# Attention's q, k and v over 128 partitions, block maxima as an operand of their own, GpSimd a pair ahead

## The chip, the core and the metric

The kernel runs on one core of one Trainium2 chip. The metric is the device time of one execution in microseconds (us), as the median of three runs. A core has TensorE (matmuls and transposes into PSUM), VectorE, ScalarE and GpSimd, each with its own queue of instructions, and SyncE, which here only issues DMAs. In rows of the profile they are called PE (with PEld for its weight loads), DVE, ACT, POOL and SP (SPq, POOLq: DMAs that they issue).

## What is computed

Three layers follow one another, all in fp32. The attention is sparse: each query sees the keys nearer than 16 positions, and one summary of each block of 32 keys.

```
B, H, S, D = 2, 8, 768, 64;  block, window = 32, 16;  nb = S // block
k_sum = k.reshape(B, H, nb, block, D).max(axis=3)
v_sum = v.reshape(B, H, nb, block, D).mean(axis=3)
scores_l = where(|i - j| < window, scale * q @ k.T, -1e9)
scores_s = scale * q @ k_sum.T + log(block)
a = softmax(concat[scores_l, scores_s]);  out = a @ concat[v, v_sum]
```

Its output (1536 rows of 512) goes through a mixture of experts that sends each row to one of 8 experts (relu between 512x1024 and 1024x512 weights), and that output through a layer `(g * cos(g)) @ w_out` with `g = x @ w_in` (512x2048 and 2048x512).

## The kernel before, in words

**The attention loop.** A pair is one batch with two heads; there are 8, four for each batch. The loop `for i in range(NH + 2)` runs over halves: half i works on pair p = i // 2, on its first 384 queries where i is even and its last where i is odd, and it overlaps stages of neighbouring halves. What each half issues, in this order (`manual_schedule`: every engine gets its instructions in the order in which the code is written):

- Even halves prepare the keys of the next pair (`prep_k`), odd ones its queries (`prep_q`). GpSimd has first reordered the loaded tile so that two heads lie side by side (`shuffle`); TensorE transposes it (tiles `pk`, `pq`); `evac_k` on ScalarE copies the windows of 96 keys for each tile of 64 queries into `kb`, and VectorE takes the block maxima `ks` from PSUM, which VectorE or GpSimd copies behind every window of `kb` (24 columns, 12 times).
- `attn_scores`: 12 matmuls of 64 queries by 96 keys and 24 maxima, then on VectorE the masked sum (`s`) and its negated maximum (`nmx`). Odd halves also multiply the value sums `va`, which GpSimd makes with three additions (`prep_v1`), for the means `vsm`.
- `attn_av` for half i - 2: products with the values, and on VectorE three operations on `rs` that divide by the sums into `xb` or `big`.
- `attn_aT` for half i - 1: six transposes into `pa`, copied by ScalarE into `aT`. Then `attn_exp` for half i: six exponentials on ScalarE.

`q`, `k` and `v` are loaded by SyncE's queue in tiles of 96 partitions with 8 rows each. There is one buffer for each; a load is issued when the reorder has read the tile before.

**Around it.** `PLAN` is a string that names, for each half and each place in it (0, p, s, c, h, e), pieces of other work: the router of the first batch (A, B, P, K, C, M, T, Q), the scatter of its rows to DRAM (Z, in half 12), and the start of the experts (W, X, from half 14). `ON_VECTOR` names copies that VectorE does in place of ScalarE or GpSimd, `EARLY` the halves in which GpSimd's work is issued ahead of the scores. When half 17 is done, the experts run (`moe_first`, `moe_window`, 7 windows), with the second batch's router between, and then the last layer (`ffn_tile`). `keep_warm` issues matmuls on zeros.

Of the kernel before, what the change touches and what calls it, by code (L numbers as in the profile page):

```python
# [34 lines left out]
QP = 96  # L35
QJ = S // QP
# [15 lines left out]
ON_VECTOR = "e2 k4 k6 k8 k12 k14 x2 x3 x5"  # L52

EARLY = (2, 12)
# [20 lines left out]
C_MASK = C_VIND + NB  # L75
# [4 lines left out]
def shape_constants():  # L80
# [4 lines left out]
    c[np.arange(QP), C_VIND + np.arange(QP) // (BLK // QJ)] = 1.0 / BLK  # L85
# [19 lines left out]
def fused_kernel(ctx, tc, q, k, v, emb, tau, w1, w2, w_in, w_out, consts, out):  # L105
# [31 lines left out]
    def load_raw(b, g, raw, which="qkv"):  # L137
        h0 = 2 * g
        for w in which:
            src, off = dict(q=(q, 0), k=(k, 2), v=(v, 0))[w]  # L140
            nc.sync.dma_start(
                raw[w + "n"][off:off + QP],
                src[b, h0:h0 + 2].rearrange("h (p j) d -> p h (j d)", p=QP),
            )
# [19 lines left out]
    def shuffle(raw, n, scale, ap, eng, r=None):  # L164

        if r is None:
            r = ap.tile([P, QJ, 2, D], F32, tag="shuf", name="shuf", bufs=1)
        r = r[0:n]
        eng.tensor_scalar(
            r.rearrange("p j h d -> p h j d"), raw.rearrange("p h (j d) -> p h j d", d=D),  # L170
            scale, 1.0, op0=ALU.mult, op1=ALU.mult,
        )
        return r

    def prep_q(bf, qs, ps_t, eng):
# [24 lines left out]
    def prep_k(bf, kr, pks, ap, eng, copy_first=False):  # L200

        kb = bf["kb"]
        n = QJ // len(pks)
        for j in range(QJ):
            nc.tensor.transpose(
                pks[j // n][:, j % n, 0:QP + 4], kr[:, j].rearrange("p h d -> p (h d)"),
                ident[0:QP + 4, 0:QP + 4],
            )
        ks = ap.tile([P, 2, NB], F32, tag="ks", name="ks")
        for m, pk in enumerate(pks):  # L210
            if copy_first:
# [9 lines left out]
        eng.tensor_scalar(  # L221
            kb[:, :, KW:KC], ks[:, 0].unsqueeze(1).to_broadcast([P, NT, NB]),
            1.0, 1.0, op0=ALU.mult, op1=ALU.mult,
        )

    def prep_v1(bf, ap, eng):
        v4 = bf["vn"].rearrange("p h (j d) -> p h j d", d=D)
        va = ap.tile([QP, 2, 4, D], F32, tag="va", name="va", bufs=1)
        eng.tensor_tensor(va, v4[:, :, 0:4, :], v4[:, :, 4:8, :], op=ALU.add)
        eng.tensor_tensor(va[:, :, 0:2, :], va[:, :, 0:2, :], va[:, :, 2:4, :], op=ALU.add)  # L230
        eng.tensor_tensor(va[:, :, 0, :], va[:, :, 0, :], va[:, :, 1, :], op=ALU.add)
        return va
# [20 lines left out]
    def attn_scores(half, bf, ps_s, ap, va=None):  # L253
        qT, kb = bf["qT"], bf["kb"]
# [3 lines left out]
        for u in range(NU // 2):  # L258
            for hh in range(2):
                for m in range(2):  # L260
                    t = NU * half + 2 * u + m
                    hp = slice(64 * hh, 64 * hh + 64)
                    nc.tensor.matmul(
                        ps[64 * m:64 * m + 64, hh, u * KC:(u + 1) * KC],
                        lhsT=qT[hp, t * 64:(t + 1) * 64], rhs=kb[hp, t, :],
                        start=True, stop=True,
                    )
        pv = ps[KW:KC, 0, 3 * KC:3 * KC + 2 * D].rearrange("p (h d) -> p h d", h=2)
# [723 lines left out]
    with ExitStack() as actx:  # L992
# [26 lines left out]
        for i in range(2):  # L1019
            s = dict(  # L1020
                raw,
                vw=[ap1.tile([P, 2, NU, D + 1], F32, name=f"vw{i}{h}") for h in range(2)],
                qT=ap1.tile([P, S], F32, name=f"qT{i}"),
                kb=ap1.tile([P, NT, KC], F32, name=f"kb{i}"),
# [18 lines left out]
        load_raw(*pairs[0], raw, "k")  # L1043
        load_raw(*pairs[0], raw, "q")
        load_raw(*pairs[0], raw, "v")
        nc.sync.dma_start(csa, consts[:, C_VIND:])

        def q_room():
            r = xp.tile([P, 2 * ROW], F32, tag="xw", name="qr", bufs=3)
            return r[:, 0:2 * QJ * D].rearrange("p (j h d) -> p j h d", j=QJ, h=2)  # L1050


        kr = shuffle(
            raw["kn"], QP + 4, 1.0, ap, nc.vector,
            sets[1]["kb"].rearrange("p t c -> p (t c)")[:, 0:2 * QJ * D].rearrange(
                "p (j h d) -> p j h d", j=QJ, h=2
            ),
        )
        load_raw(*pairs[1], raw, "k")
        qs = shuffle(raw["qn"], QP, SCALE, ap, nc.vector)  # L1060
        load_raw(*pairs[1], raw, "q")
        load_vw(*pairs[0], 0, sets[0]["vw"][0])
# [6 lines left out]
        prep_k(sets[0], kr, two_banks(), ap, nc.gpsimd)  # L1069
        prep_q(sets[0], qs, ps_t, nc.vector)  # L1070
        keep_warm(6, P)
        va = prep_v1(raw, ap, nc.vector)
        load_raw(*pairs[1], raw, "v")
        kr = shuffle(raw["kn"], QP + 4, 1.0, ap, nc.gpsimd)
        load_raw(*pairs[2], raw, "k")
        qs1 = shuffle(raw["qn"], QP, SCALE, ap, nc.gpsimd, q_room())
        load_raw(*pairs[2], raw, "q")
        load_vw(*pairs[0], 1, sets[0]["vw"][1])

# [78 lines left out]
        for i in range(NH + 2):  # L1158
            def prep_qv():
                nonlocal qs, va  # L1160
                qs = shuffle(raw["qn"], QP, SCALE, ap, nc.gpsimd, q_room())
                va = prep_v1(raw, ap, nc.vector if f"v{i}" in on_vector else nc.gpsimd)
                if p + 2 < NPR:
                    load_raw(*pairs[p + 2], raw, "qv")

# [10 lines left out]
            if i == 7:  # L1176
                zt = xp.tile([P, ROW], F32, tag="junk", name="zt")
# [9 lines left out]
            if nx is not None and not odd and i > 2:  # L1187
                pk = ps_t.tile([P, QJ, P], F32, tag="tr", name="pk")
                prep_k(
                    nx, kr, [pk], ap, nc.vector if f"k{i}" in on_vector else nc.gpsimd,  # L1190
                    f"e{i}" in on_vector,
                )
# [3 lines left out]
            if i in EARLY:  # L1196
                prep_qv()
# [6 lines left out]
            if i == 0:  # L1204
                prep_v3(sets[0], means_v(va))
                va = prep_v1(raw, ap, nc.gpsimd)
                load_raw(*pairs[2], raw, "v")
                load_vw(*pairs[1], 0, sets[1]["vw"][0])
            if i == 1:
                prep_q(nx, qs1, ps_t, nc.scalar)  # L1210
# [228 lines left out]
```

## Time and profile before

| | |
|---|---|
| median of 3 runs | 539.37 us (537.84 to 540.14) |
| the profiled execution | 539.12 us, its span 537.3 us |
| TensorE busy | 506.7 us, 94% of the span |
| VectorE, ScalarE, GpSimd busy | 404.3, 304.0, 107.6 us |
| granted TensorE clock, mean | 0.984 |
| first expert's first matmul | at 97.98 us |

The span runs from the first instruction to the last; the execution has 1.8 us more around it. Busy shares are means over the attention (to about 97 us, every engine with gaps) and the two dense layers behind it, where TensorE has none.

### The profile page before, as it was taken

What the parts mean: (1) busy time and instruction counts of PE and PEld (TensorE: products, weight loads), DVE (VectorE), ACT (ScalarE), POOL (GpSimd) and SP (SyncE); (2) the same over time, 40 slices, a digit from 0 to 9 for tenths busy, and PEclk for the clock granted to TensorE, in tenths of its full rate; (3) what the DMA queues carried; (4) which work ended last, traced back from release to release, by engine and by line L of the source; (5) the groups of instructions that cost most, each with busy time, mean ns of one, the idle gap of its engine ahead of it and who ended that gap; (6) DMA issues with size and microseconds to landing.
All of it is one profiled execution on the core that took longest, in us unless ns stands there. A gap on an engine that the chain in (4) does not pass through costs nothing. (4 is left out here: it accounts for less than half of the span.)

```text
span 537.3 us, 10198 instructions
## 1 busy us (share of the span) xinstructions
PE 506.7 (94%) x3748; PEld 459.7 (86%) x3748; DVE 404.3 (75%) x834; ACT 304.0 (57%) x642; POOL 107.6 (20%) x134
## 2 busy tenths in 40 slices
PE   7879977899999999999999999999999999999993
PEld 6657656679999999999999999999999999999992
DVE  5689784898768688889779998976699765655562
ACT  2778865997656556566557675633364433333330
POOL 3787574751534000000000000000000000001222
PEclk9999986999999999999999999999999999999998
DMA  8999747787797566766304433220010000001111
GB/s 213 243 206 253 176 109 254 266 285 244 247 333 259 160 209 219 234 197 199 119 2 137 138 117 119 78 79 0 1 40 2 1 0 1 0 2 59 60 59 63
DMA packets 47688, 72.31 MB, mean 135 GB/s; under 512 B 21256, under 2 KB 21512, under 8 KB 47632
## 3 DMA queue, kind: packets, MB, share of 16 engines
q1 hardware_dynamic: 44800, 62.11, 39.6%
q0 software_dynamic: 2832, 9.49, 5.0%
q8 instruction: 31, 0.51, 0.4%
q14 instruction: 25, 0.20, 0.1%
HBM read 64.22 MB, written 7.37 MB: 133 GB/s over the span
## 5 line engine op out<-in xcount | busy, mean ns | idle before, releaser
L720 PE MATMUL po<-sl,gt 128*128 128x512 f32 x567 | 139.8, 391 | 0.0
L720 PEld LDWEIGHTS po<-sl,gt 128*128 128x128 f32 x567 | 105.5, 188 | 18.2
L720 PE MATMUL ph<-yT,sl 128*128 128x384 f32 x576 | 107.7, 336 | 0.0
L720 PEld LDWEIGHTS ph<-yT,sl 128*128 128x128 f32 x576 | 101.2, 188 | 3.7
L630 DVE TENSOR_TENSOR sl<-raw,sl 128x512 fp32r<-128x512 f32 x112 | 75.0, 706 | 11.3 <-ACT sl L629 10.9
L973 POOL DMA_INDIRECT out_dram<-acc,perm x12 | 12.0, 998 | 345.1 <-DVE acc L1349 342.6
L720 PE MATMUL py<-ht,sl 128*128 128x256 f32 x576 | 73.8, 284 | 0.0
L629 ACT ACTIVATE sl<-raw 128x512 fp32r<-128x512 f32 x112 | 63.5, 625 | 17.5 <-PE py L720 12.3
L720 PE MATMUL ph<-xT,sl 128*128 128x256 f32 x576 | 72.3, 282 | 1.0 <-DVE ht L816 1.0
L720 PEld LDWEIGHTS ph<-xT,sl 128*128 128x128 f32 x576 | 69.7, 188 | 2.4 <-DVE ht L816 1.4
L720 PEld LDWEIGHTS py<-ht,sl 128*128 128x128 f32 x576 | 70.4, 188 | 0.9 <-issue 0.6
L930 ACT ACTIVATE u<-u 128x384 f32<-128x384 f32 x64 | 33.6, 525 | 62.9 <-DVE u L929 62.8
L934 ACT ACTIVATE gt<-t 128x384 fp32r<-128x384 f32 x63 | 33.0, 524 | 31.3 <-DVE t L933 31.1
L926 ACT ACTIVATE t<-ph 128x384 f32<-128x384 f32 x64 | 31.3, 488 | 31.6 <-PE ph L720 31.2
L933 DVE TENSOR_TENSOR t<-ph,u 128x384 f32<-128x384 f32 (+1 forms) x66 | 35.8, 544 | 17.7 <-ACT u L930 17.5
L935 DVE TENSOR_TENSOR gt<-t,gt 128x384 fp32r<-128x384 f32 x63 | 35.1, 557 | 17.2 <-ACT gt L934 16.6
L928 DVE TENSOR_SCALAR u<-t 128x384 f32<-128x384 f32 x64 | 23.0, 359 | 27.7 <-ACT t L926 27.2
L929 DVE TENSOR_TENSOR u<-t,u 128x384 f32<-128x384 f32 x64 | 35.6, 557 | 1.1
L720 PE MATMUL ph<-yT,early 128*128 128x384 f32 x192 | 36.1, 338 | 0.2 <-DVE yT L1296 0.2
L720 PEld LDWEIGHTS ph<-yT,early 128*128 128x128 f32 x192 | 33.9, 188 | 1.7 <-DVE yT L1296 0.5
L284 ACT ACTIVATE s<-s,nmx 128x120 f32<-128x120 f32 x96 | 29.0, 385 | 2.6 <-DVE nmx L279 1.5
L815 ACT ACTIVATE ht<-ph 128x256 fp32r<-128x256 f32 x48 | 17.8, 378 | 15.9 <-PE ph L720 15.9
(189 smaller groups left out, 652.8 us busy)
## 6 DMA issues: line engine op xcount, KB each, us to landing
raw<-in_moe_w_dram SPq DMA_DIRECT2D x56, 512.0 KB, 4.1
raw<-in_moe_w_in_dram SPq DMA_DIRECT2D x16, 512.0 KB, 3.7
raw<-in_moe_w_out_dram SPq DMA_DIRECT2D x16, 512.0 KB
vw<-in_v_dram SPq DMA_DIRECT2D x32, 120.0 KB, 6.1
xw<-xs POOLq DMA_DIRECT2D x6, 516.0 KB
kn<-in_k_dram SPq DMA_DIRECT2D x8, 384.0 KB, 4.6
qn<-in_q_dram SPq DMA_DIRECT2D x8, 384.0 KB, 5.0
vn<-in_v_dram SPq DMA_DIRECT2D x8, 384.0 KB, 5.8
```

Source lines behind the costliest of these rows:

```text
L284: nc.scalar.activation(s[:, u, :], s[:, u, :], AF.Exp, bias=nmx[:, u:u + 1])
L629: nc.scalar.activation(sl[:, 0, c], r, AF.Copy)
L630: nc.vector.tensor_tensor(sl[:, 1, c], r, sl[:, 0, c].bitcast(F32), op=ALU.subtract)
L720: nc.tensor.matmul(acc, lhsT=lw(a), rhs=lx(c), start=(first and i == 0), stop=(last and i == 2))
L815: nc.scalar.activation(ht[:, 0], ph, AF.Relu)
L926: nc.scalar.activation(t, ph, AF.Copy, scale=1.0 / TWO_PI, bias=0.25)
L928: nc.vector.tensor_scalar(u, t, ROUND, -ROUND, op0=ALU.add, op1=ALU.add)
L929: nc.vector.tensor_tensor(u, t, u, op=ALU.subtract)
L930: nc.scalar.activation(u, u, AF.Sin, scale=TURN)
L933: nc.vector.tensor_tensor(g, ph[:, cs], u[:, cs], op=ALU.mult)
L934: nc.scalar.activation(gt[:, 0], g, AF.Copy)
L935: lo = nc.vector.tensor_tensor(gt[:, 1], g, gt[:, 0].bitcast(F32), op=ALU.subtract)
```

## The change

- q, k and v are loaded over 128 partitions with 6 rows each (768 = 128 * 6), k and v into two buffers each and q into three, and the reorders write tiles of their own (`kr`, `qs`, `va`). GpSimd's reorders and sums are issued for pair p + 2 where the prepared pair is p + 1, and the next loads behind them.
- The transposed keys go into one copy `kT` of 768 columns with 16 zero columns at either end. A tile's window is a slice of it (`kT[hp, t * 64:t * 64 + KW]`), so the scores are 12 matmuls by 96 columns.
- The block maxima are taken from `kT` in SBUF into `ks`, which is the operand of six further matmuls of 128 queries by 24 columns each half. No copy of them is made.
- The scale of q is applied in the copy out of PSUM, not in the reorder. For pair 0, keys and queries aren't reordered: 12 matmuls with the identity turn each.
- The value sums are one addition of neighbouring rows, and three matmuls where there was one.
- ScalarE gets the exponentials of half i ahead of `aT` of half i - 1. `qT` of halves 3, 5, 7 and 13 is copied by VectorE; `kT` by ScalarE in all halves but the first two, where VectorE and ScalarE take half each. Zeros for the padding rows (`zt`) move from half 7 to half 10.

`PLAN` stays.

```diff
-ON_VECTOR = "e2 k4 k6 k8 k12 k14 x2 x3 x5"
-
-EARLY = (2, 12)
+ON_VECTOR = "q3 q5 q7 q13 x2 x3 x5"
...
+    def turn_heads(dst, src, j, raw):
+
+        if not raw:
+            nc.tensor.transpose(dst, src[:, j].rearrange("p h d -> p (h d)"), ident)
+            return
+        for hh in range(2):
+            nc.tensor.matmul(
+                dst[64 * hh:64 * hh + 64], lhsT=src[:, hh, j * D:(j + 1) * D], rhs=ident,
+                start=True, stop=True,
+            )
+
+    def natural(dst, pk, j0, j1, scale, eng):
+
+        dst = dst.rearrange("d (p j) -> d p j", j=QJ)[:, :, j0:j1]
+        src = pk.rearrange("d j p -> d p j")
+        if eng is nc.scalar:
+            nc.scalar.activation(dst, src, AF.Copy, scale=scale)
+        else:
+            eng.tensor_scalar(dst, src, scale, 1.0, op0=ALU.mult, op1=ALU.mult)
...
-        ks = ap.tile([P, 2, NB], F32, tag="ks", name="ks")
-        for m, pk in enumerate(pks):
-            if copy_first:
-                evac_k(kb, pk, m * n, (m + 1) * n, nc.scalar)
-            nc.vector.tensor_reduce(
-                ks[:, m], pk[:, :, 2:2 + QP].rearrange("d j (n r) -> d n r j", r=BLK // QJ),
-                axis=AX.XY, op=ALU.max,
-            )
-            if not copy_first:
-                evac_k(kb, pk, m * n, (m + 1) * n, nc.scalar)
-        if len(pks) == 2:
-            nc.vector.tensor_tensor(ks[:, 0], ks[:, 0], ks[:, 1], op=ALU.max)
-        eng.tensor_scalar(
-            kb[:, :, KW:KC], ks[:, 0].unsqueeze(1).to_broadcast([P, NT, NB]),
-            1.0, 1.0, op0=ALU.mult, op1=ALU.mult,
-        )
...
+            turn_heads(pks[j // n][:, j % n], kn, j, raw)
+        kT = bf["kT"][:, WIN:WIN + S]
+        for m, (pk, eng) in enumerate(zip(pks, engs)):
+            natural(kT, pk[:, 0:n], m * n, (m + 1) * n, 1.0, eng)
+        nc.vector.tensor_reduce(
+            bf["ks"], kT.rearrange("d (n r) -> d n r", r=BLK), axis=AX.X, op=ALU.max
+        )
...
-                        ps[64 * m:64 * m + 64, hh, u * KC:(u + 1) * KC],
-                        lhsT=qT[hp, t * 64:(t + 1) * 64], rhs=kb[hp, t, :],
+                        ps[64 * m:64 * m + 64, hh, u * KC:u * KC + KW],
+                        lhsT=qT[hp, t * 64:(t + 1) * 64], rhs=kT[hp, t * 64:t * 64 + KW],
                         start=True, stop=True,
                     )
+        for u in range(NU // 2):
+            for hh in range(2):
+                t = NU * half + 2 * u
+                hp = slice(64 * hh, 64 * hh + 64)
+                nc.tensor.matmul(
+                    ps[:, hh, u * KC + KW:(u + 1) * KC],
+                    lhsT=qT[hp, t * 64:(t + 2) * 64], rhs=ks[hp, :], start=True, stop=True,
+                )
...
-                prep_k(
-                    nx, kr, [pk], ap, nc.vector if f"k{i}" in on_vector else nc.gpsimd,
-                    f"e{i}" in on_vector,
-                )
+                pk = ps_t.tile([P, 8, P], F32, tag="tr", name="pk")
+                prep_k(nx, kr, [pk], [nc.vector if f"k{i}" in on_vector else nc.scalar])
+                shuffle_k(p + 2)
             elif nx is not None and odd and i > 1:
-                prep_q(nx, qs, ps_t, nc.scalar)
+                prep_q(nx, qs, ps_t, nc.vector if f"q{i}" in on_vector else nc.scalar)
+                shuffle_q(p + 2)
...
             if 0 <= i - 1 < NH:
-                aTs[i - 1] = attn_aT(ss.pop(i - 1), ps_a, ap, i)
+                pa = attn_turn(ss.pop(i - 1), ps_a)
             if i == 1:
                 keep_warm(4, P, ps_s, "s")
             if i < NH:
                 attn_exp(s, nmx)
...
+            if 0 <= i - 1 < NH:
+                aTs[i - 1] = attn_aT(pa, ap, i)
```

What the engines get in another order is seen best from half 3 to half 4. On VectorE, before: the division of half 3 (`rs`), the maxima of the next pair's keys straight from PSUM (`pk`), their copy into `kb`, then half 4's masked sum and its maximum.

```order
L313 TENSOR_SCALAR rs<-po 128x6
L314 RECIPROCAL rs<-rs 128x6
L316 TENSOR_TENSOR xb_209<-po,rs 128x3x128
L213 TENSOR_REDUCE ks<-pk 128x24
L221 TENSOR_SCALAR kb_132<-ks 128x12x24
L272 TENSOR_TENSOR s<-ps,csa 128x720
L279 TENSOR_REDUCE nmx<-s 128x6
```

Now the same place:

```order
L304 TENSOR_SCALAR rs<-po 128x6
L305 RECIPROCAL rs<-rs 128x6
L307 TENSOR_TENSOR xb_218<-po,rs 128x3x128
L203 TENSOR_REDUCE ks_136<-kT_135 128x24
L260 TENSOR_TENSOR s<-ps,csa 128x720
L267 TENSOR_REDUCE nmx<-s 128x6
```

The copy into `kb` is gone, and the maxima read `kT_135`, which ScalarE writes, in place of `pk`. They still stand ahead of the masked sum.

On ScalarE, before: `aT` of half 2, the exponentials of half 3, the windows of the next pair's keys, `aT` of half 3, the exponentials of half 4.

```order
L296 ACTIVATE aT<-pa 120x768
L284 ACTIVATE s<-s,nmx 128x120 x6
L196 ACTIVATE kb_132<-pk 128x12x96
L296 ACTIVATE aT<-pa 120x768
L284 ACTIVATE s<-s,nmx 128x120 x6
```

Now, from the means of half 3 on:

```order
L223 ACTIVATE vsm<-ps 24x128
L272 ACTIVATE s<-s,nmx 128x120 x6
L287 ACTIVATE aT<-pa 120x768
L185 ACTIVATE kT_135<-pk 128x768
L272 ACTIVATE s<-s,nmx 128x120 x6
L287 ACTIVATE aT<-pa 120x768
```

The keys' copy stands behind the exponentials of half 3 as before, and `aT` of half 2 now stands between the two.

On GpSimd, before: the work for pair 3's queries and values in half 4, then pair 4's keys.

```order
L248 TENSOR_SCALAR vw_126<-vsm 24x12x64
L169 TENSOR_SCALAR qr<-qn 96x2x8x64
L229 TENSOR_TENSOR va<-vn 96x512
L230 TENSOR_TENSOR va<-va 96x2x128
L231 TENSOR_TENSOR va<-va 96x2x64
L355 TENSOR_TENSOR en<-en,half_t 8x1
L169 TENSOR_SCALAR shuf<-kn 100x2x8x64
```

Now, from half 3 on (`qs` and `va` of pair 3, then the keys of pair 4, which half 6 transposes):

```order
L163 TENSOR_SCALAR qs<-qr 128x2x6x64
L209 TENSOR_TENSOR va<-vn 128x2x3x64
L228 TENSOR_SCALAR vw_127<-vsm 24x12x64
L228 TENSOR_SCALAR vw_128<-vsm 24x12x64
L163 TENSOR_SCALAR kr<-kn_113 128x2x6x64
L346 TENSOR_TENSOR en<-en,half_t 8x1
```

Each reorder now stands behind the transposes of the pair before and about two halves ahead of its own.

## Rows read from the trace of the kernel before

**Rows 1.** Busy time by stretch: start:end, length, each engine's busy us, clock, DMA.

```profile
40.00:50.00 10.00, 8.99 (x164) 7.69 (x163) 9.40 (x17) 8.74 (x20) 8.95 (x12) 1.00 1.03 266
...
80.00:90.00 10.00, 8.28 (x104) 6.39 (x103) 4.06 (x8) 4.76 (x14) 3.66 (x5) 0.52 0.78 260
...
350.00:400.00 50.00, 50.00 (x256) 45.56 (x255) 35.68 (x71) 22.77 (x44) 0.00 (x0) 1.00 0.10 32
```

**Rows 2.** Timeline, 76 to 103 us: start, length, engine, line, operation, [idle before <-releaser].

```profile
76.37 1.23 POOL L542 DMA_INDIRECT xs<-xb,posi  x1 [1.88 <-DVE rs L313]
...
80.16 1.48 PE L263 MATMUL ps<-kb,qT 64*64 64x120 f32 x24
...
93.07 0.69 POOL L764 TENSOR_SCALAR xw<-xw 128x512 f32<-128x512 f32 x1
...
94.94 0.94 PE L307 MATMUL po<-vw,aT 120*64 120x65 f32 x24 [0.34 <-issue]
...
95.81 0.66 PE L778 MATMUL px<-cst,xw 128*128 128x128 f32 x4
...
97.98 4.81 PE L720 MATMUL h<-sl,xT 128*128 128x512 f32 x18 [1.08 <-DVE xT L781]
```

**Rows 3.** Timeline, from the maximum of half 3 to that of half 5.

```profile
26.80 0.90 DVE L279 TENSOR_REDUCE nmx<-s 128x6 f32<-128x720 f32 x1
...
28.51 1.81 ACT L284 ACTIVATE s<-s,nmx 128x120 f32<-128x120 f32 x6
...
29.28 0.91 PE L205 MATMUL pk<-cst,shuf 100*128 100x100 f32 x8 [1.76 <-POOL shuf L169]
...
30.30 0.96 DVE L213 TENSOR_REDUCE ks<-pk 128x24 f32<-128x768 f32 x1 [1.71 <-PE pk L205]
...
31.29 0.93 DVE L221 TENSOR_SCALAR kb<-ks 128x288 f32<-128x288 f32 x1
...
32.14 0.89 DVE L272 TENSOR_TENSOR s<-ps,csa 128x720 f32<-128x720 f32 x1
...
33.06 0.90 DVE L279 TENSOR_REDUCE nmx<-s 128x6 f32<-128x720 f32 x1
...
36.17 0.90 DVE L279 TENSOR_REDUCE nmx<-s 128x6 f32<-128x720 f32 x1
```

**Rows 4.** Timeline of VectorE, the maxima of halves 1, 7, 9, 11 and 12.

```profile
16.23 0.90 DVE L279 TENSOR_REDUCE nmx<-s 128x6 f32<-128x720 f32 x1
...
45.32 0.90 DVE L279 TENSOR_REDUCE nmx<-s 128x6 f32<-128x720 f32 x1
...
52.97 0.90 DVE L279 TENSOR_REDUCE nmx<-s 128x6 f32<-128x720 f32 x1
...
66.86 0.90 DVE L279 TENSOR_REDUCE nmx<-s 128x6 f32<-128x720 f32 x1
...
72.78 0.90 DVE L279 TENSOR_REDUCE nmx<-s 128x6 f32<-128x720 f32 x1
```

**Rows 5.** Groups by line, 0 to 140 us: count | busy us, mean ns | idle before.

```profile
L296 ACT ACTIVATE aT<-pa 120x768 f32<-120x768 f32 x16 | 13.0, 810 | 10.8 <-PE pa L291 10.7
...
L184 ACT ACTIVATE qT<-pq 128x768 f32<-128x768 f32 x7 | 5.5, 792 | 0.0
...
L186 DVE COPY qT<-pq 128x768 f32<-128x768 f32 x1 | 1.0, 957 | 0.5 <-PE pq L178 0.5
```

**Rows 6.** Timeline of TensorE up to the first scores.

```profile
6.36 1.60 PE L205 MATMUL pk<-cst,kb 100*128 100x100 f32 x8 [0.69 <-DVE kb L169]
...
9.03 2.51 PE L1013 MATMUL pw<-still 128*128 128x128 f32 x12
...
11.47 0.84 PE L263 MATMUL ps<-kb,qT 64*64 64x120 f32 x24
```

**Rows 7.** Timeline of ScalarE, the last row square of half 11.

```profile
69.20 0.19 ACT L406 ACTIVATION_READ_ACCUMULATOR junk<-xb 128x1 f32 x1
```

**Rows 8.** DMA issues, 0 to 140 us: count, KB each, median us to landing.

```profile
raw<-in_moe_w_dram SPq DMA_DIRECT2D x24, 512.0 KB, 4.4
...
kn<-in_k_dram SPq DMA_DIRECT2D x8, 384.0 KB, 4.6
```

More of the change, by code (lines that the diff above doesn't have):

```diff
@@ L135, in fused_kernel, with load_raw @@
     SCALE = 1.0 / math.sqrt(D)
[L137 to L143, printed above, removed]
-            )
+    def load_raw(src, b, g, dst):
+        nc.sync.dma_start(
+            dst, src[b, 2 * g:2 * g + 2].rearrange("h (p j) d -> p h (j d)", p=P)
+        )
     def load_vw(b, g, half, vw):
@@ L241, in evac_v, with prep_v1, prep_v2 @@
+    def prep_v1(vn, va, eng):
+        v5 = vn.rearrange("p h (j t d) -> p h j t d", t=2, d=D)
+        eng.tensor_tensor(
+            va.rearrange("p j h d -> p h j d"), v5[:, :, :, 0, :], v5[:, :, :, 1, :], op=ALU.add
+        )
+    def prep_v2(va, pv):
+        for j in range(NV):
+            nc.tensor.matmul(
+                pv, lhsT=csa[:, j * NB:(j + 1) * NB], rhs=va[:, j],
+                start=j == 0, stop=j == NV - 1,
+            )
     def evac_v(pv, ap):
@@ L1042, in fused_kernel, with load_q, load_k, load_v @@
         NPR = len(pairs)
[L1043 to L1061 removed]
+        for s in sets:
+            for c0 in (0, WIN + S):
+                nc.vector.memset(s["kT"][:, c0:c0 + WIN], 0.0)
+        qns = {}
+        def load_q(n):
+            r = xp.tile([P, 2 * ROW], F32, tag="xw", name="qr", bufs=3)
+            qns[n] = r[:, 0:2 * QJ * D].rearrange("p (h c) -> p h c", h=2)
+            load_raw(q, *pairs[n], qns[n])
+        def load_k(n):
+            load_raw(k, *pairs[n], kns[n % 2])
+        def load_v(n):
+            load_raw(v, *pairs[n], vns[n % 2])
+        def shuffle_k(n):
+            if n < NPR:
+                shuffle(kns[n % 2], krt, nc.gpsimd)
+            if n + 2 < NPR:
+                load_k(n + 2)
+        def shuffle_q(n):
+            if n < NPR:
+                shuffle(qns.pop(n), qst, nc.gpsimd)
+            if n + 1 < NPR:
+                load_q(n + 1)
+        def pair_v(n, eng):
+            if n < NPR:
+                prep_v1(vns[n % 2], va, eng)
+            if n + 2 < NPR:
+                load_v(n + 2)
+        kr, qs = (t.rearrange("p (j h d) -> p j h d", h=2, d=D) for t in (krt, qst))
+        load_k(0)
+        load_q(0)
+        nc.sync.dma_start(csa, consts[:, C_VIND:])
+        load_v(0)
+        load_k(1)
+        load_q(1)
         load_vw(*pairs[0], 0, sets[0]["vw"][0])
+        load_v(1)
         def two_banks():
@@ L1205, in fused_kernel @@
                 prep_v3(sets[0], means_v(va))
-                va = prep_v1(raw, ap, nc.gpsimd)
-                load_raw(*pairs[2], raw, "v")
+                pair_v(1, nc.gpsimd)
                 load_vw(*pairs[1], 0, sets[1]["vw"][0])
             if i == 1:
-                prep_q(nx, qs1, ps_t, nc.scalar)
+                prep_q(nx, qs, ps_t, nc.scalar)
+                shuffle_q(2)
             if i == 2:
-                pk = ps_t.tile([P, QJ, P], F32, tag="tr", name="pk")
-                prep_k(nx, kr, [pk], ap, nc.gpsimd, f"e{i}" in on_vector)
+                pk = ps_t.tile([P, 8, P], F32, tag="tr", name="pk")
+                prep_k(nx, kr, [pk], [nc.scalar])
+                shuffle_k(3)
+            if nx is not None and odd and i > 1:
+                pair_v(p + 2, nc.gpsimd)
             at(i, "c")
```

130 lines of the change are left out of this document (42 added, 88 removed).

## Prediction

> **What bounds the kernel now.** I read three views: the busy time in stretches of 10 us, then the timeline from 75 to 98 us, then the timeline of the attention before it. In the late part TensorE is busy for the whole of every stretch [rows 1], and the change does not touch that part. The first matmul of the first expert starts at 97.98 us [rows 2], so what follows takes 537.3 - 97.98 = 439.3 us, and I carry it over unchanged. The question is only when that matmul starts.
>
> It stands at the end of two chains. One is the scatter of the first batch's rows: the first scatter starts at 76.37 us, and the rows come back, gated, at 93.07 + 0.69 = 93.76 us, 17.4 us later [rows 2]. The other is the rest of the attention: its last product starts at 94.94 us and the turn of the gated rows follows at 95.81 us [rows 2]. The second ends last, by 2.05 us. Both hang on the time at which half 12 of the attention is reached, since the plan hands the scatter out there.
>
> Within the attention I use one mark for each half: the end of its negated maximum on VectorE, called N. From the rows N1 = 17.13, N3 = 27.70, N4 = 33.96, N5 = 37.07, N7 = 46.22, N9 = 53.87, N11 = 67.76 and N12 = 73.68 us [rows 3, 4]. A pair thus takes 10.57, 9.37, 9.15 and 7.65 us from N1 to N9. In the pair from N3 to N5 the reader sees why: TensorE waits 1.76 us for GpSimd's reordered keys, the block maximum starts behind the transposes at 30.30, and the copy into kb and the masked sum queue behind it on VectorE [rows 3]. From an even half to the next odd one it goes fast: N4 to N5 is 3.11 us.
>
> **The change, part by part.**
>
> *The waits on GpSimd go.* Keys and queries are reordered a pair ahead, the value sums need one addition where they needed three, and GpSimd no longer copies maxima. The 1.76 us of [rows 3] go. So does VectorE's kb copy of 0.93 us.
>
> *A new wait comes in the same place.* The maximum (ks) is now taken from kT in SBUF, and kT is written by ScalarE. In ScalarE's order the kT of half 4 stands behind the exponentials of half 3 and behind aT; on VectorE the masked sum of half 4 stands behind ks. So from the odd N to the even N everything is in a row: exponentials 1.81 [rows 3], aT 0.81, kT 0.79 (priced as the qT copy of the same 768 columns) [rows 5], ks 0.95 (0.96 from PSUM [rows 3]), masked sum 0.90, maximum 0.90 [rows 3]. The sum is 6.16; neighbours on one engine overlap by about 0.1 and handoffs cost about as much, so 6.15. Before, this leg took 33.96 - 27.70 = 6.26 us, and there it consisted of stalls. Queued behind the waiting ks are the masked sum, the maximum, the three operations on rs and then qT; the exponentials of the half wait for them, which closes the circle.
>
> *qT moves to VectorE in halves 3, 5, 7 and 13.* It costs 0.957 us there [rows 5], between the even and the odd maximum. The odd leg was 3.11 with 0.3 of waiting; with qT it is 3.8 (3.6 if all the waiting was hidden, 4.1 if none). In half 9, qT stays on ScalarE and the leg is 3.15. A pair is then 6.15 + 3.8 = 9.95 us, and 9.3 for the one that ends with half 9. Against 9.37, 9.15 and 7.65 that is +0.6, +0.8 and +1.65, together **+3.05** (2.3 to 3.9).
>
> *The start.* The first keys and queries are turned without a reorder, in 12 matmuls each where 8 transposes took 1.60. The keep-warm matmuls are the nearest row: six in 2.51 us, 0.42 each [rows 6]. As two matmuls write different halves of the partitions I take 2.5 us for each dozen, between 1.6 (like the transposes) and 5.0 (one after the other). Keys that are there at 5.6 us (6.36 less the reorder of 0.7) give 5.6 + 2.5 + 2.5 + 1.5 (keep-warm) = 12.1 for the first scores, where they start at 11.47 [rows 6]; between 10.3 and 14. Six further matmuls on the maxima lengthen the scores from 0.84 to about 1.3 (0.84 to 1.7). Then half 1 has the new circle too: 1.3 + 0.9 + 0.9 + 1.81 + 0.5 (half of kT) + 0.95 + 0.9 + 0.9 = 8.2, so N1 = 20.3 in place of 17.13. From there the second batch of keep-warm matmuls, which needs the scores' PSUM tile, waits for the masked sum: N1 - 0.9 + 1.1 + 0.6 + 1.3 + 1.8 = N1 + 3.9 for N2, and ks, rs, qT, masked sum, maximum and 0.4 of waits, 5.1 more, to N3 = 29.3. That is **+1.6** (-0.2 to +3.2).
>
> *Half 9 to half 11.* The router's copies and logits stand between the halves in both kernels (13.89 us before). The exponentials of half 9 now go ahead of aT; kT and ks fall where VectorE has router work to do. I take **-0.3** (-1 to +1).
>
> *Half 11 to half 12.* Three row squares on ScalarE end at 69.39 us, 1.63 after N11 [rows 7], and the exponentials start behind them. New chain: 1.63 + 6.15 + 0.4 of small VectorE work - 0.2 of overlap = 8.0 where 5.92 were needed: **+2.1** (1.5 to 2.5).
>
> *Half 12 to the first expert.* VectorE's qT in half 13 adds 0.96. That the exponentials no longer wait for aT takes about as much off. **0** (-2.05, if the attention stops being the later of the two chains, to +1.5).
>
> *TensorE's own load and the loads.* In 40 to 50 us TensorE is busy 8.99 of 10 [rows 1], 8.2 us in a pair of 9.15. Twelve more small matmuls a pair and two on the value sums bring that to 8.4 to 9.6, below 9.95: nothing, as long as the new circle is longer. The same holds for the loads: keys and queries now arrive a pair ahead of need, so faster loads earn nothing.
>
> **Sum.** 1.6 + 3.05 - 0.3 + 2.1 + 0 = 6.45 us. The profiled execution took 539.12 us (span 537.3 and 1.8 around it); the median is 0.25 above it. 539.12 + 6.4 gives **545.5 us**. The low bounds of all terms add to 0.6, the high ones to 12.2; they will not all fall together, so 542.1 to 549.5 is this case's own range.
>
> **Rivals.** Half a per cent of the median, 2.7 us, is about what can be told from no change: below 536.7 is faster, above 542.1 slower.
>
> *The circle is there, but most is given back.* The start comes at its low bound (-0.2), the tail at its own (-2.05), the rest stays: 3.05 - 0.3 + 2.1 - 2.25 = +2.6 at most, +1 with the low pair bounds. 540 to 541.7 us, no change. For it: the scatter chain has 2.05 us of room. Against: nothing in the change speeds the half-clock stretch in which the tail runs.
>
> *Faster: GpSimd and the loads were what set the pace.* The point that decides is whether kT is written when VectorE reaches ks. If it is, no circle closes, and every pair runs like the one without a GpSimd stall, 7.65 us: 3 x 7.65 = 22.95 for 26.17 (-3.2), about -1.6 between N1 and N3, -1.1 for the kb copy between N11 and N12, together -5.9 or 533.2 us. For it: the 1.76 us of waiting [rows 3], and that 512 KB over 128 partitions land in 4.4 us where 384 KB of keys over 96 take 4.6 [rows 8]. Against: VectorE comes to ks some 2.3 us before kT can end, in every pair, and neither a quicker load nor a quicker GpSimd moves ScalarE's exponentials. The Trainium skill, page "SBUF — State Buffer", section "Door 1: The DMA port swizzle", says that partitions 0 to 63 reach only the even half of the 16 ports, so that a tile of 96 loads them unevenly. By that rule the loads come sooner and the time falls as in this rival; the trace agrees on the loads, and it shows no wait that they would still shorten once they are a pair ahead.
>
> *TensorE's clock falls a second time.* From 80 to 90 us the granted clock is 0.52 [rows 1], 1.2 GHz for most of it, after a stretch with gaps, and scores that took 0.84 take 1.48 [rows 2, 6]. If the new waits bring that into the loop, a pair needs 8.2 x 1.48 / 0.84 = 14.4 us for 9.95: 4.4 more, 550 us.
>
> **How the numbers follow.** The circle as summed: 0.62. Given back: 0.15. Faster: 0.13. Second fall of the clock: 0.10. The range 538 to 550.5 leaves out the faster rival and part of the last, about 0.2. Faster by over 0.5%: 0.13; within: 0.16; slower: 0.71.
>
> **What would show it.** In the profile after: each even half's ks on VectorE idle before it for 2 us or more, released by ScalarE's kT; pairs near 10 us between odd maxima; no wait of TensorE for GpSimd; N12 near 80 us; the first expert's matmul near 104.5. I am wrong if kT ends before VectorE gets to ks, if ks is much shorter from SBUF, or if the pairs fall below 8.5 us.

## The result and the profile after

The changed kernel takes **545.3 us** (median of 4 runs, 544.65 to 546.41), the kernel before 538.6 us beside it (537.76 to 540.14): ratio 1.0123, 95% interval 1.0091 to 1.0156. That is slower by 1.2%, with the whole interval above 1, and the forecast was 545.5 us. The profiled execution took 545.71 us, its span is 544.03 us for 537.27. Medians are over all runs; ratios, here and below, leave out the few runs in a slower state.

A table by stage comes first, made from the ends of the `nmx` rows (N) and the start of the first expert's matmul, as in the prediction. The total is right, but several of its stages are not: the first expert's matmul comes 10.0 us later, where 6.45 were forecast, and 3.2 us that no one forecast come back behind it.

| us | before | after | difference | forecast |
|---|---|---|---|---|
| N1 | 17.13 | 18.21 | +1.1 | +3.2 |
| N1 to N3 | 10.57 | 11.08 | +0.5 | -1.6 |
| N3 to N9 | 26.17 | 28.90 | +2.7 | +3.05 |
| N9 to N11 | 13.89 | 16.29 | **+2.4** | **-0.3** |
| N11 to N12 | 5.92 | 7.86 | +1.9 | +2.1 |
| N12 to the first expert | 24.30 | 25.62 | +1.3 | 0 |
| from there to the end | 439.3 | 436.1 | **-3.2** | **0** |

The timeline of VectorE and ScalarE after, from the maximum of half 3 to that of half 5, answers to [rows 3]:

```profile
28.38 0.90 DVE L267 TENSOR_REDUCE nmx<-s 128x6 f32<-128x720 f32 x1
...
29.32 1.82 ACT L272 ACTIVATE s<-s,nmx 128x120 f32<-128x120 f32 x6 [0.59 <-DVE nmx L267]
...
31.17 0.81 ACT L287 ACTIVATE aT<-pa 120x768 f32<-120x768 f32 x1
31.87 0.81 ACT L185 ACTIVATE kT<-pk 128x768 f32<-128x768 f32 x1
32.71 0.95 DVE L203 TENSOR_REDUCE ks<-kT 128x24 f32<-128x768 f32 x1 [2.54 <-ACT kT L185]
33.58 0.90 DVE L260 TENSOR_TENSOR s<-ps,csa 128x720 f32<-128x720 f32 x1
34.52 0.90 DVE L267 TENSOR_REDUCE nmx<-s 128x6 f32<-128x720 f32 x1
...
36.29 0.94 DVE L187 TENSOR_SCALAR qT<-pq 128x768 f32<-128x768 f32 x1
37.15 0.90 DVE L260 TENSOR_TENSOR s<-ps,csa 128x720 f32<-128x720 f32 x1
...
38.08 0.90 DVE L267 TENSOR_REDUCE nmx<-s 128x6 f32<-128x720 f32 x1
```

Read it from the maximum that ends at 29.28: exponentials, aT and kT follow one another on ScalarE, and VectorE, idle for 2.54 us, takes ks at 32.71 and only then the masked sum. The next maximum ends at 35.42, 6.14 us later. The three pairs take 9.70, 9.74 and 9.47 us. In half 12 the same row shows once more, behind ScalarE's squares:

```profile
79.44 0.95 DVE L203 TENSOR_REDUCE ks<-kT 128x24 f32<-128x768 f32 x1 [3.62 <-ACT kT L185]
```

The waits after, for 28 to 84 us: engine, line, what it waited for, us in total, times, longest.

```profile
DVE ks L203 <- ACT kT L185: 10.8, 5, 3.6
...
PE po L298 <- ACT aT L287: 3.9, 3, 1.7
PE pxa L365 <- ACT aT L287: 1.3, 1, 1.3
PE po L298 <- POOL vw L228: 0.9, 1, 0.9
```

TensorE waits for ScalarE's aT now; its wait for GpSimd's keys [rows 3] is gone from the pairs. Its start answers to [rows 6]:

```profile
5.05 1.79 PE L175 MATMUL pk<-cst,kn 128*64 128x128 f32 x24
6.68 1.48 PE L175 MATMUL pq<-cst,qr 128*64 128x128 f32 x24
8.08 1.61 PE L1005 MATMUL pw<-still 128*128 128x128 f32 x12
9.62 0.73 PE L243 MATMUL ps<-kT,qT 64*64 64x96 f32 x24
10.27 0.85 PE L252 MATMUL ps<-ks,qT 64*128 64x24 f32 x12
```

The raw turns cost 1.79 and 1.48 us and not 2.5 each, and the first scores start 1.85 us earlier than in [rows 6]. That lead is not the change's: the kernel before, profiled a second time, has

```profile
8.12 1.53 PE L1013 MATMUL pw<-still 128*128 128x128 f32 x12
```

and its first scores at 9.58 us. The 2.51 us that the same six matmuls took in [rows 6], from which the forecast took 0.42 us each, belong to that one profile. Its first record of the granted clock, at full, is at 11.06 us, that of the second profile at 6.54. The windows of the same stretches as in [rows 1], and of the new half-clock stretch:

```profile
40.00:50.00 10.00, 9.12 (x159) 7.94 (x157) 8.32 (x17) 6.32 (x18) 7.07 (x9) 1.00 0.94 225
...
100.00:110.00 10.00, 8.21 (x68) 6.83 (x69) 5.31 (x11) 6.19 (x13) 5.64 (x8) 0.56 0.60 218
350.00:400.00 50.00, 50.00 (x256) 45.65 (x255) 35.66 (x72) 21.47 (x43) 0.00 (x0) 1.00 0.13 40
```

The tail, where [rows 2] stood, in the timeline:

```profile
84.66 1.23 POOL L533 DMA_INDIRECT xs<-xb,posi  x1 [6.99 <-DVE rs L304]
...
100.44 0.99 PE L298 MATMUL po<-vw,aT 120*64 120x65 f32 x24 [2.71 <-ACT aT L287]
...
101.50 0.68 POOL L755 TENSOR_SCALAR xw<-xw 128x512 f32<-128x512 f32 x1
...
103.90 1.59 PE L298 MATMUL po<-vw,aT 120*64 120x65 f32 x24 [0.79 <-issue]
...
105.43 1.12 PE L769 MATMUL px<-cst,xw 128*128 128x128 f32 x4
...
107.96 6.04 PE L711 MATMUL h<-sl,xT 128*128 128x512 f32 x18 [0.56 <-DVE xT L772]
```

The gated rows are there at 102.18, 17.5 us after the first scatter (17.4 before), and the attention's last product still ends the later of the two chains.

### The profile page after: what moved, and what is told of

Its sections match the earlier page's. It is cut to its first block, busy times and chain, and to the rows that moved or that the text cites. A ratio compares the mean times of both kernels' runs of the same rounds, so it can differ in the third digit from the quotient of the medians.

```text
span 544.0 us, 10623 instructions
## 1 busy us (share of the span) xinstructions
PE 514.8 (95%) x3976; PEld 470.7 (87%) x3976; DVE 397.5 (73%) x829; ACT 298.9 (55%) x637; POOL 92.3 (17%) x116
## 5 line engine op out<-in xcount | busy, mean ns | idle before, releaser
L621 DVE TENSOR_TENSOR sl<-raw,sl 128x512 fp32r<-128x512 f32 x112 | 73.4, 692 | 13.4 <-ACT sl L620 13.1
L711 PE MATMUL py<-ht,sl 128*128 128x256 f32 x576 | 71.8, 282 | 0.0
L620 ACT ACTIVATE sl<-raw 128x512 fp32r<-128x512 f32 x112 | 63.6, 627 | 14.9 <-PE py L711 11.5
L711 PEld LDWEIGHTS py<-ht,sl 128*128 128x128 f32 x576 | 68.7, 188 | 0.6 <-issue 0.6
L924 DVE TENSOR_TENSOR t<-ph,u 128x384 f32<-128x384 f32 (+1 forms) x66 | 35.6, 543 | 17.7 <-ACT u L921 17.5
L272 ACT ACTIVATE s<-s,nmx 128x120 f32<-128x120 f32 x96 | 29.1, 382 | 18.6 <-DVE nmx L267 10.3
L711 PEld LDWEIGHTS ph<-yT,early 128*128 128x128 f32 x192 | 33.8, 188 | 1.7 <-DVE yT L1302 0.5
L806 ACT ACTIVATE ht<-ph 128x256 fp32r<-128x256 f32 x48 | 18.1, 379 | 17.1 <-PE ph L711 16.8
```

Source lines behind the costliest of these rows:

```text
L272: nc.scalar.activation(s[:, u, :], s[:, u, :], AF.Exp, bias=nmx[:, u:u + 1])
L620: nc.scalar.activation(sl[:, 0, c], r, AF.Copy)
L621: nc.vector.tensor_tensor(sl[:, 1, c], r, sl[:, 0, c].bitcast(F32), op=ALU.subtract)
L711: nc.tensor.matmul(acc, lhsT=lw(a), rhs=lx(c), start=(first and i == 0), stop=(last and i == 2))
L806: nc.scalar.activation(ht[:, 0], ph, AF.Relu)
L924: nc.vector.tensor_tensor(g, ph[:, cs], u[:, cs], op=ALU.mult)
```

## The experiments

The first four ran in one session, the next four in a second on the same chip, and the last four in a third on another chip, each with the kernel before beside them (538.38, 539.62 and 538.30 us). Ratios are to that kernel. N marks are those of one profiled execution of each kernel.

**Block maximum behind the half's own maximum.**

```
-prep_k(nx, kr, [pk], [...])                # kT, then ks
+prep_k(nx, kr, [pk], [...], ks=False)      # kT alone
 s, nmx, vsm = attn_scores(...)
+if nx is not None and not odd and i > 2: block_max(nx)
```

> Circle theory (ScalarE's kT, with the block maximum standing ahead of the masked sum on VectorE, sets the even legs): nothing on VectorE's path waits for kT any more. Pairs from N3 to N9 fall from 9.7 us to what TensorE's own work leaves, 8.4 to 8.8 (28.9 -> 25.8, -3.1), N11 to N12 from 7.85 to about 6.0 (-1.9), N9 to N11 from 16.3 to about 15.3 (-1): 545.3 - 6.0 = 539.3 us (538 to 541.5). Rival A (TensorE's added matmuls, six on the maxima in each half and three on the value sums, are what lengthens a pair): the same work stands on TensorE, pairs stay at 9.5 or more, 545 us. Rival B (GpSimd's reorder or the loads): no change, 545 us.

Measured 541.47 us, ratio 1.0057 (1.0024 to 1.0090). The even legs fell to 3.87, 4.03 and 4.28 us, so the wait for kT is what made them 6.14. The odd legs rose to 5.40, 5.57 and 5.03, and the pairs only fell to 9.27, 9.60 and 9.32. Of the 5.2 us that this profile is ahead of the changed kernel's at N12, only 0.7 come from the three pairs; half 9 to half 11 gave 1.3 and half 11 to half 12 gave 2.7. Of the 6 us forecast in the total 2 did not come, and TensorE's timeline in the pair from half 5 to half 7 shows where they went:

```profile
37.69 0.82 PE L172 MATMUL pk<-cst,kr 128*128 128x128 f32 x6
38.44 0.73 PE L248 MATMUL ps<-kT,qT 64*64 64x96 f32 x24
39.10 0.85 PE L257 MATMUL ps<-ks,qT 64*128 64x24 f32 x12
40.78 0.97 PE L303 MATMUL po<-vw,aT 120*64 120x65 f32 x24 [0.83 <-ACT aT L292]
41.68 0.41 PE L360 MATMUL pe<-cst,big 8*128 8x8 f32 x4
42.02 0.87 PE L284 MATMUL pa<-cst,s 128*120 128x128 f32 x6
42.73 0.82 PE L172 MATMUL pq<-cst,qs 128*128 128x128 f32 x6
43.48 0.73 PE L248 MATMUL ps<-kT,qT 64*64 64x96 f32 x24
44.14 0.85 PE L257 MATMUL ps<-ks,qT 64*128 64x24 f32 x12
44.92 0.84 PE L221 MATMUL ps<-va,csa 128*24 128x128 f32 x6
45.69 0.97 PE L303 MATMUL po<-vw,aT 120*64 120x65 f32 x24
```

TensorE now has hardly a gap but the 0.83 us in which it waits for aT, which stands behind the exponentials on ScalarE. A second limit lies 0.1 to 0.4 us below the first.

**kT on VectorE, qT back on ScalarE.**

```
-ON_VECTOR = "q3 q5 q7 q13 x2 x3 x5"
+ON_VECTOR = "k4 k6 k8 k10 k12 x2 x3 x5"
```

> Circle theory: kT written by VectorE waits for TensorE's transposes only. Even leg 0.96 (kT) + 0.95 (ks) + 0.9 + 0.9 + 0.9 (three operations on rs) = 4.6 in place of 6.14; odd leg 3.1 to 3.6, as qT goes back to ScalarE; the pair is then TensorE's 8.4 to 8.8. N11 to N12 about 6.0. 539.5 us (538 to 541.5). Rival A (TensorE's load): no change, 545 us. Rival C (VectorE is short of time itself, so what stands in it sets the pace): kT costs it 0.96 and qT gives back 0.96, no change, 545 us.

541.27 us, ratio 1.0032 (0.9995 to 1.0069). The pairs are 9.34, 9.67 and 9.39, N11 to N12 is 5.14. VectorE waits for kT no longer; its largest wait is for TensorE's scores and value sums. Another way to break the circle, and the same second limit.

**aT ahead of the exponentials.**

```
+aTs[i - 1] = attn_aT(pa, ap, i)
 attn_exp(s, nmx)
-aTs[i - 1] = attn_aT(pa, ap, i)
```

> Circle theory: with aT ahead of the exponentials again, the row from odd to even maximum loses aT: 1.81 + 0.79 + 0.95 + 0.90 + 0.90 = 5.35 in place of 6.14, -0.8 in each of three pairs, and -0.8 from N11 to N12; 545.3 - 3.2 = 542 us (541 to 543.5). It falls short of that where aT waits for TensorE's turn of the half before and so holds the exponentials up. Rivals A and B (TensorE, GpSimd): no change, 545 us.

541.37 us, ratio 1.0043 (1.0018 to 1.0069): the total is as forecast, its parts are not. The pairs fell to 9.36, 9.11 and 8.75: -0.34, -0.63 and -0.72 where 0.8 was the whole length of aT. N11 to N12 stayed at 7.85: there the exponentials stand behind the squares, and kT behind both, in either order. A half-clock stretch from 63.6 to 67.1 us took its N9 to N11 to 17.30. Its profile is only 1.6 us ahead of the changed kernel's at N12; another 2.4 us of its gain lie behind N12, where none was forecast.

**The matmuls on the maxima twice in even halves.**

```
 nc.tensor.matmul(ps[...], lhsT=qT[...], rhs=ks[hp, :], ...)
+if half == 0: nc.tensor.matmul(ps[...], lhsT=qT[...], rhs=ks[hp, :], ...)
```

> The six matmuls on the block maxima run twice in every even half (same result). Circle theory: in the even halves the masked sum waits for the block maximum, 2.5 us, so 0.85 us more on TensorE ahead of it costs nothing in the loop; +0.8 in half 0 only, where no such wait stands: 546.1 us (545 to 547). Rival A (TensorE's load sets the pairs): +0.85 in each pair from N1 to N12, six of them, and half 0: 550 to 551 us.

546.99 us, ratio 1.0140 (1.0097 to 1.0183). Two of the pairs did not move (9.69, 9.46), one took 0.7 more (10.44). So in the pairs the added work on TensorE lies under the wait for kT, nearly all of it. From N9 to N10, where the router's matmuls stand between, 10.93 us for 10.25: the masked sum waited 1.44 us for TensorE there, 0.76 in the changed kernel, so it costs 0.7 of its 0.85. N9 to N11 took 18.08 us, and a half-clock stretch from 68.7 to 72.1 us lies between N10 and N11. The start came 1.5 us later at N1, of which 0.8 were there before the first doubled matmul.

**Late block maximum and aT first, together.** The two diffs above.

> Block maximum behind the half's maximum on VectorE, and aT ahead of the exponentials on ScalarE. Theory now: two limits lie close together, the circle (9.7 us a pair, gone here) and TensorE's row (8.5 us of work a pair and 0.9 of waiting for aT, which stood behind the exponentials; the wait goes here). Pairs 8.5 to 8.8 in place of the 9.3 to 9.6 of the run with the late block maximum alone, -2.3 over three pairs: 541.5 - 2.3 = 539 us (537 to 540.5). Rival (the circle was all, and the pairs of 9.4 are set by something on VectorE): no further gain, 541.5 us.

540.99 us, ratio 1.0028 (1.0002 to 1.0055). The pairs are 9.06, 8.60 and 8.15, 2.4 us less over three than with the late maximum alone, as forecast. The median is half a microsecond lower than that of the late maximum alone, which ran in another session; against the kernel before of its own session each is slower, by 3.1 us there and 1.4 here. In the profiled execution the part behind the first expert's matmul took 442.3 us, where other kernels took 435 to 439; TensorE waits there, once for 2.43 us, for a copy by ScalarE (`ht`). Over its 12 runs the kernel scattered from 538.8 to 545.4.

**The same without the matmuls on the maxima.** The block scores are left out: the scores read 120 columns of keys, as many as before, and the last 24 stand in their place.

```
-rhs=kT[hp, t * 64:t * 64 + KW]     # 96 columns
+rhs=kT[hp, t * 64:t * 64 + KC]     # 120 columns
-ps[:, hh, u * KC + KW:(u + 1) * KC], lhsT=qT[...], rhs=ks[hp, :]     # six
```

> As the run before, but the matmuls on the block maxima are left out, and the score matmuls read 120 columns of keys in place of 96, as wide as in the kernel before: the block scores are wrong ones. Theory (TensorE's added 0.85 us in each half is the limit that is left): pairs 8.5 -> 7.5 (-1.0 each, bounded by VectorE's and ScalarE's 7 to 7.5), N9 to N11 -1.2, -0.7 in half 0 and half 1, -0.5 from N11 on: about -6 from the run before it, 533 us (531 to 535.5). Rival (TensorE's added work is hidden): no change from the run before it, 539 us.

535.12 us, ratio 0.9920 (0.9892 to 0.9947): 5.9 us below the run with both edits. The pairs are 8.16, 8.08 and 7.10. N9 to N11 fell from 15.03 to 13.75. Up to N12 the profile is 3.8 us ahead of that of both edits (70.40 for 74.17 us), and this is what the maxima on TensorE cost in the loop once the circle is gone; the rest of the 5.9 lies behind N12 and was not forecast there.

**The kernel before, with the maximum taken from ScalarE's copy.**

```
+if len(pks) == 1:
+    evac_k(kb, pk, m * n, (m + 1) * n, nc.scalar)
+    nc.vector.tensor_reduce(ks[...], kb[:, :, WIN:WIN + 64]..., op=ALU.max)
+    continue
```

> The kernel before, with one part of the change alone: in the loop the block maximum is taken from ScalarE's copy of the keys in SBUF, not from PSUM. Circle theory: the row exponentials 1.81, copy 1.13, ks 0.95, copy into kb 0.93, masked sum 0.90, maximum 0.90 = 6.6 closes in every even half; with odd legs of 3.1 the pairs are 9.7 where they were 9.37, 9.15 and 7.65 (+2.9), N11 to N12 1.63 + 6.6 = 8.2 for 5.9 (+2.3): 538.6 + 5 = 543.5 us (541 to 546). Rival A (TensorE's added work alone makes the change slower): TensorE has the same work as before, 538.5 us.

550.19 us, ratio 1.0199 (1.0173 to 1.0225). TensorE and GpSimd have the work of before, and this one part costs more than the whole change, and more than the 541 to 546 us forecast. The profile is that of the fastest of its five runs, 546.35 us, and has N12 at 81.74 us for 73.68. The pairs took 9.99, 10.69 and 9.42 us. Half 6, in the timeline:

```profile
38.21 0.81 ACT L304 ACTIVATE aT<-pa 120x768 f32<-120x768 f32 x1 [0.28 <-PE pa L299]
...
38.92 1.81 ACT L292 ACTIVATE s<-s,nmx 128x120 f32<-128x120 f32 x6
...
40.63 1.11 ACT L196 ACTIVATE kb<-pk 128x1152 f32<-128x1152 f32 x1
41.77 0.95 DVE L215 TENSOR_REDUCE ks<-kb 128x24 f32<-128x768 f32 x1 [2.87 <-ACT kb L196]
42.76 0.31 DVE L229 TENSOR_SCALAR kb<-ks 128x288 f32<-128x288 f32 x1
42.99 0.90 DVE L280 TENSOR_TENSOR s<-ps,csa 128x720 f32<-128x720 f32 x1
```

The same circle, and longer than the 6.6 us forecast, since in the order of before aT stands inside it, ahead of the exponentials, and TensorE, whose turn aT waits for, ran at half the clock from 35.8 to 42.6: 7.72 us in this half. The legs into halves 4 and 8 took 7.29 and 6.77.

**GpSimd's reorders twice.**

```
 eng.tensor_scalar(r..., raw..., 1.0, 1.0, ...)
+if twice: eng.tensor_scalar(r..., raw..., 1.0, 1.0, ...)      # from pair 2 on
```

> The changed kernel with each of GpSimd's two reorders of a pair done twice (from pair 2 on): 1.66 us more on GpSimd a pair. Circle theory: GpSimd is a pair ahead and has 3 us free in each pair, so nothing: 545.3 us (544.5 to 546). Rival B (GpSimd sets the pace): up to +1.66 a pair, seven pairs or less: 550 us and more.

552.88 us, ratio 1.0234 (1.0203 to 1.0264). Neither theory has that. The pairs are 9.70, 9.74 and 9.47, N9 to N11 16.29: to 0.02 us those without the doubling, so in the loop GpSimd sets nothing. The 4.0 us stand between N1 and N3 (15.12 for 11.08). TensorE's timeline:

```profile
22.19 0.87 PE L284 MATMUL pa<-cst,s 128*120 128x128 f32 x6
25.79 1.54 PE L177 MATMUL pq<-cst,qs 128*128 128x128 f32 x6 [2.73 <-POOL qs L168]
27.26 1.24 PE L248 MATMUL ps<-kT,qT 64*64 64x96 f32 x24
28.43 1.48 PE L257 MATMUL ps<-ks,qT 64*128 64x24 f32 x12
29.84 1.47 PE L221 MATMUL ps<-va,csa 128*24 128x128 f32 x6
```

In half 3 TensorE does wait for GpSimd's queries, 1.13 us in the first profile of the changed kernel and 2.73 here, and GpSimd waits for their load. Behind that wait the granted clock is 0.5 from 25.8 to 32.6 us, 1.2 GHz, and the rows take 1.24 for 0.73 and 1.48 for 0.85. The other 5 us of this profile lie behind N12, with 20.5 us at the half clock in three stretches between 83.8 and 118.0; why those fell there stays open.

**Queries loaded two pairs ahead.**

```
-if n + 1 < NPR: load_q(n + 1)
+if n + 2 < NPR: load_q(n + 2)      # and load_q(2) ahead of the loop
```

> The changed kernel with the queries loaded two pairs ahead in place of one, so that GpSimd's reorder for half 3 no longer waits for its load. Theory: in the start the loads, not the circle, set the leg from N1 to N3 (TensorE waits 1.13 us there for the reordered queries): 11.1 -> 9.9 to 10.1, nothing in the pairs behind it; 545.3 - 1.1 = 544.2 us. Rival (TensorE's row is full there, another wait takes its place): 11.1 stays, 545.3 us.

547.33 us, ratio 1.0170 (1.0133 to 1.0207); the changed kernel itself took 547.42 in the same session, in one run. N1 to N3 is 9.73, TensorE waits for no reordered queries there, and N3 to N5 rose to 11.19. That the early load made the leg shorter is not shown by its length: the run with the late maximum, without the early load, has no such wait either and the same 9.73 us, with TensorE's row in half 3 without a gap. In the second profile of the changed kernel the wait is 0.56 us and the leg 10.50, and N3 stands at 28.18 us, earlier than the 28.43 here. VectorE's timeline in half 5 has the wait that took its place:

```profile
34.89 0.56 DVE L307 TENSOR_TENSOR xb<-po,rs 128x384 f32<-128x384 f32 x1
36.86 0.16 DVE L347 RECIPROCAL tauc<-tauc 128x1 f32<-128x1 f32 x1 [1.41 <-DMA tauc<-in_moe_tau_dram]
36.94 0.94 DVE L187 TENSOR_SCALAR qT<-pq 128x768 f32<-128x768 f32 x1
```

A load of 0.5 KB for the router, issued in half 3 behind the loads of v, now ends last; qT and the masked sum are queued behind it, and a half-clock stretch from 37.3 to 40.7 us follows.

**All three together.**

> Late block maximum, aT ahead of the exponentials, and the queries loaded two pairs ahead. Theory: start to N3 1 us shorter than with the first two (28.2 -> 27.2), pairs 8.1 to 9.0 as there, the rest as there but for the clock: 541 - 1 = 540 us, within 0.5% of the kernel before. Rival (start hidden): 541 us.

538.25 us, ratio 1.0000 (0.9963 to 1.0036). The time of before is reached, not beaten. It ran on another chip than the run with two edits. N1 to N3 is 9.72, but N1 came later in this profile, so N3 stands at 28.32 where the run with two edits had 28.18; the pairs are 8.35, 8.69 and 8.35, 0.4 less in sum. Its profile ends 7.0 us before that of the two edits, and 5.3 of them lie behind the first expert's matmul (437.0 for 442.3), which the early queries do not explain.

**The two kernels once more.**

> The kernel before, profiled once more. If the 3.3 us that the part behind the first expert's matmul took less in the changed kernel (436.1 for 439.3) belong to the change, this profile shows 439.3 within 0.5 again; if they are scatter from run to run, it may show anything from 435 to 442.

541.86 us in one run. Its N3 to N9 took 27.00 us for 26.17: two half-clock stretches (13.4 to 16.8 and 30.4 to 33.8 us) that the first profile does not have. Behind the first expert's matmul 438.7 us, within the 0.6 of the first.

> The changed kernel, profiled once more: N marks within 0.2 us of those of its first profile up to N12 (82.3), and 436 us behind the first expert's matmul if that part belongs to the change; another value from 435 to 442 if it is scatter.

547.42 us in one run. Pairs 9.70, 9.74 and 9.47, N9 to N11 16.29, as at first; only the start is shorter, so N12 is 81.24, 1.1 us from the forecast that allowed 0.2. N3 stands at 28.18 us, and in the second profile of the kernel before at 28.20. Behind the first expert's matmul 437.1 us.

## Why the prediction was right, step by step

**The total is right in good part by luck.** Up to the first expert's matmul +6.45 us were forecast and +10.0 measured: half 9 to half 11 is 2.7 us over its forecast and the tail 1.3. The part behind that matmul, which the prediction had put at nothing, gave 3.2 back. Of the signs that it named, the idle time ahead of ks (2.54 us) and the pairs near 10 us came; N12 stood at 82.3 for 80 and the first expert's matmul at 108.0 for 104.5, and TensorE still waited for GpSimd, 1.13 us in half 3 and 0.9 for `vw`.

**The circle**, the mechanism of the forecast, is shown. Where ks is late and where kT moves to VectorE, the even legs shorten; where aT leaves the circle, the legs and the pairs do; and each edit takes about 4 us off the total. Put into the kernel before, the circle costs 2% by itself. The leg was forecast at 6.15 us and measured 6.14, 6.14 and 6.20. **Odd legs**: 3.56, 3.60 and 3.27 for 3.8, 3.8 and 3.15. **N11 to N12**: +1.9 for +2.1.

**TensorE's own load: "nothing, as long as the new circle is longer"** held in the pairs, where doubling the matmuls on the maxima moved one of three. What it did not say is how near the second limit is: 9.3 to 9.6 us a pair with the wait for aT, the upper end of the 8.4 to 9.6 that it gave. So no edit to the circle alone earns the kernel of before back.

**The step that failed: "Half 9 to half 11 ... -0.3 (-1 to +1)".** It measured +2.4. The prediction let the copy of keys and the maximum fall where VectorE has router work, and put nothing on TensorE there. In this stretch TensorE has its attention work and the router's turns and logits: the busy time in it, before and after, is

```profile
53.87:67.76 13.89, 12.66 (x188) 9.62 (x184) 10.62 (x25) 11.23 (x28) 8.03 (x10) 1.00 0.75 180
```

```profile
58.19:74.48 16.29, 15.37 (x227) 12.13 (x226) 10.92 (x25) 11.27 (x30) 5.30 (x8) 1.00 0.34 103
```

with 91 and 94% of it on TensorE. The runs split the 2.4 us: 16.29 falls to 15.03 with the late maximum (1.26 us were the wait for kT), and to 13.75 without the matmuls on the maxima (1.28 us were TensorE's work), where the kernel before has 13.89.

**The start: +1.6 forecast, +1.6 measured, by luck.** Two errors cancel: the raw turns and the maxima were dearer in the forecast (N1 +3.2, measured +1.1; the first scores at 9.62, outside its 10.3 to 14), and the leg to N3 (-1.6, measured +0.5) was thought free of waits for GpSimd. That "the waits on GpSimd go" was true of the keys in the pairs and not of the queries in half 3. And the +1.6 is that of one pair of profiles: in the second pair N3 stands at the same place in both kernels, 28.20 and 28.18 us.

**"I carry it over unchanged": 439.3 forecast, 436.1 measured.** Kernels built on the one before took 439.3, 438.7 and 439.1 us behind the first expert's matmul, the last of them with that matmul at 105.7 us, so that its coming later is not by itself what shortens this part; the changed kernel and its variants took 435.3 to 437.2 in eight of eleven profiles, and 438.8, 439.2 and 442.3 in the others. Some 2 us thus go with the change more often than not. In the first profile of before TensorE stands 1.73 us in gaps of over 0.1 us there, in that of after 0.41; but in the second profile of before it is 0.62, with 438.7 us, so the gaps are not all of it. Why, was not tried; it stays open.

**The tail: 0 forecast, +1.3.** The granted clock was at half for 13.7 us before (75.9 to 89.6) and for 3.4 and 10.2 us after (91.0 to 94.4, 101.2 to 111.4), the last of which covers the first expert. Up to its matmul that is 13.7 us at half before and 10.2 after, so the clock alone does not make the tail longer. The prediction took it that the exponentials, which no longer wait for aT, give back what qT costs. What it left out is that aT now stands behind them: TensorE's longest wait in the tail is the 2.71 us for aT ahead of 100.44, where before it is 2.13 us. But with aT first a wait of 2.67 us, for GpSimd's `vw`, stands in the same place, so the cause of the +1.3 stays open. Where the half-clock stretches fall differs from run to run: one lies from 89.6 to 113.5 in the second profile of the changed kernel, which took 1.8 us more from N12 to the first expert.

**Rivals.** *Given back*: the start and the tail did not come at their low bounds; but 2 to 3 us did come back, behind the first expert, where the prediction had not looked. *Faster, GpSimd and the loads set the pace*: not in the loop, by the doubled reorders; in half 3 they can, as there. *Second fall of the clock*: not inside the loop of the changed kernel, in either profile, but in that of four of its variants, with the doubled reorders, the earlier queries, aT first and the doubled matmuls.

## What to carry to other kernels

When an operand moves from PSUM to a copy in SBUF, the copying engine joins the path of whoever reads it: look up what stands ahead of the copy in that engine's order, and what stands behind the reader in the other's. Price every limit of a loop and not only the longest, because the next one decides what a repair is worth: here one circle of 9.7 us hid a row of 9.4. A stage that shares an engine with other work (the router here) has its own limit, so work that is free in the loop may cost its full length there. And take a price from more than one profile: six keep-warm matmuls took 2.51 us in one and 1.53 in the next.

## What the hardware showed that was not expected

Twelve matmuls that each write 64 of 128 output partitions took 1.79 and 1.48 us, 0.12 to 0.15 us each (1.53 and 1.51 in the second profile), where six on all partitions and of the same 128 columns took 1.61 us, 0.27 each. Two that write different halves together cost about as much as one.

The loads of keys over 128 partitions did not land sooner, nor did those of queries (6.4 us for 5.0); those of values took 5.6 for 5.8. DMA issues from 0 to 140 us after: count, KB each, median us to landing; before, over 96 partitions, the keys took 4.6 [rows 8].

```profile
kn<-in_k_dram SPq DMA_DIRECT2D x8, 384.0 KB, 5.7
```

By the Trainium skill, page "SBUF — State Buffer", section "Door 1: The DMA port swizzle", a tile on all partitions loads the ports evenly, and the prediction said the trace agreed on the loads, from weights over 128 partitions beside keys over 96. With the keys themselves over 128 it does not. The loads stand behind each other in the queue, and no run here takes the layout apart from that.

A single wait of TensorE of 2.73 us was followed by 6.8 us at the half clock, in a leg of 15.12 us. In the first profile of the changed kernel the wait was 1.13 us, the clock stayed at full, and the leg was 11.08: 1.6 us more of waiting, 4.0 more of leg.
